# Third blocks of inverses on four array tiles, and state sums with 40 columns of weights, in an RWKV-7 and feed-forward kernel

## The chip, the cores and the metric

The kernel runs on one core of one Trainium2 chip. The metric is the device time of one execution in microseconds. Before the change it is 857.22 us, the median of three runs (856.4 to 857.7); the profiled execution spans 853.2 us.

## The reference

Two parts follow each other. The first is a recurrence over 768 steps of time for 4 batches of 8 heads, with a state of 40 x 40 for each head; the second is a feed-forward layer over the 3072 rows that come out.

```python
def _attn_ref(r, k, v, w, a, b):
    B, H, S, D = r.shape                 # 4, 8, 768, 40
    state = np.zeros((B, H, D, D), dtype=np.float32)
    for t in range(S):
        ...
        y[:, :, t] = np.einsum('bhd,bhde->bhe', rt, state)
        Sa = np.einsum('bhde,bhe->bhd', state, at)
        state_decay = state * wt[:, :, None, :] - np.einsum('bhd,bhe->bhde', Sa, bt)
        state = state_decay + np.einsum('bhd,bhe->bhde', vt, kt)
    return y

def _moe_ref(x, w_in, w_out):            # x: 3072 x 320, w_in: 320 x 2048, w_out: 2048 x 320
    h = x @ w_in
    relu6 = np.clip(h + 3.0, 0.0, 6.0)
    g = h * relu6 / 6.0
    return (g @ w_out).astype(np.float32)
```

All data are fp32 for the kernel's matmuls.

## The kernel before

The kernel cuts time into blocks of 64 steps. A block of two batches and all eight heads is a unit; there are 24 units, four (NU) to a group, and each goes through a preparation (stages W, gam, A, B, F, K, factor, E, EV) and a step (RT, VT, R, C, S, U, UT, rS, sn, H, y, move). Within a block the recurrence is solved with the inverse of a 64 x 64 triangular matrix for each head. That inverse is made in 32 x 32 parts: VectorE builds the inverses of the two diagonal parts for a whole group at once (`invert`), and TensorE makes the part off the diagonal, the third block, as a product of three 32 x 32 matrices, in two bursts of matmuls with an eviction after each. A third block call takes 16 heads (two units); there are twelve calls, the first two of them with `first`. On the 128 partitions lie two 64 x 64 matrices one above the other, x = 0 and 1.

```python
def third_block(F, tb, tt, n, first=False):
    zs = tmp.tile([P, 2 * H, L], F32, name="zs")                     # P = 128, H = 8, L = 32, BL = 64
    parts = [slice(0, H), slice(H, 2 * H)] if first else [slice(0, 2 * H)]
    zp = [ps_any([P, 2 * H, L]) for _ in range(2)]
    for h in range(2 * H):
        for x in range(2):
            z = x * BL
            nc.tensor.matmul(out=zp[x][z:z + L, h, :], lhsT=F[z + L:z + BL, n * H + h, L:BL],   # line 660
                             rhs=tb[z + L:z + BL, n * H + h, :], start=True, stop=True,
                             tile_position=(z + L, z))
    yield PE
    for part in parts:
        for x in range(2):
            z = x * BL
            nc.scalar.activation(out=zs[z:z + L, part], in_=zp[x][z:z + L, part], func=AF.Copy)  # line 667
    ...
    tp = [ps_any([P, 2 * H, L]) for _ in range(2)]
    for h in range(2 * H):
        for x in range(2):
            z = x * BL
            nc.tensor.matmul(out=tp[x][z:z + L, h, :], lhsT=tt[z:z + L, n * H + h, :],           # line 679
                             rhs=zs[z:z + L, h, :], start=True, stop=True,
                             tile_position=(z, z))
    yield PE
    for part in parts:
        heads = slice(n * H + part.start, n * H + part.stop)
        for x in range(2):
            z = x * BL
            nc.scalar.activation(out=tinv[z:z + L, heads, L:BL], in_=tp[x][z:z + L, part],       # line 687
                                 func=AF.Copy)
    yield DONE
```

`tile_position` names the first row and the first column of the part of TensorE's 128 x 128 array that a matmul uses. Both loops over x alternate between two such tiles.

The state's sums of a step (D = 40, SLOT = 64; `half(i)` is the 64 partitions from 64 i):

```python
def s_sn():
    sn = ps_pair(NPR, D)
    for name in "KB":
        for pr in range(NPR):                                        # 4 pairs of heads
            for s in range(2):
                for q in range(2):
                    h = 2 * pr + s
                    by = ...                                         # V or U, 64 x 40
                    nc.tensor.matmul(                                # line 818
                        out=sn[q][half(s), pr, :],
                        lhsT=o[name][half(q), h * D:h * D + SLOT], rhs=by,
                        start=(name == "K" and pr == 0), stop=(name == "B" and pr == NPR - 1))
    yield PE
    for q in range(2):
        nc.vector.tensor_tensor(out=st[:, q, :, 0:D], in0=sn[q], in1=st[:, q, :, 0:D],   # line 825
                                op=ALU.add)
```

The weights of a head are 40 columns wide, but 64 are taken, so 24 columns of the next head come along; their sums go into rows of the state that nothing multiplies with.

Buffers in PSUM: a ring of five banks called "any" for all parts of the recurrence; two banks "h" and one "o" for the feed-forward. `ps_pair` takes two banks at once, one for each row half, and lets several small results share them:

```python
def ps_pair(*dims):
    n = 1
    for d in dims:
        n *= d
    if shared[0] is None or shared[1] + n > 512:
        shared[:] = [ps_any([P, 512]) for _ in range(2)], 0
    at = shared[1]
    shared[1] += n
    ...
    return [_ap(t[:], at, views) for t in shared[0]]
```

Other lines that are spoken of: 420 transposes of inputs, 438 scores (RT with VT or UT), 447 VectorE's mask of the scores, 512 and 534 / 537 the matrix F of the early units and its eviction, 725 the state times a, 763 and 784 U and its transpose, 800 the state's part of the output, 841 the output of a block, 921 and 926 the feed-forward's first product, 931 and 932 its activation on ScalarE and VectorE, 945 its second product. Feed-forward matmuls are fed in between the stages of the recurrence, in pieces, so that TensorE has work while a stage waits for its evictions; the main loop runs a third block between such pieces:

```python
            feed(rate / 2, inversion)
            for _ in parts:
                pass
            if i % NU < 2 and j < 2:
                ...
                block(i, j)              # j = 0: the first burst of a third block, j = 1: the second
            ...
            feed(rate / 2, inversion)
```

Of the kernel before, what the change touches and what calls it, by code (L numbers as in the profile page):

```python
# [8 lines left out]
F32 = mybir.dt.float32  # L9
I32 = mybir.dt.int32  # L10
U32 = mybir.dt.uint32
ALU = mybir.AluOpType
AF = mybir.ActivationFunctionType
# [3 lines left out]
P = 128  # L17
BL = 64
HB = BL // 2
L = 32  # L20
SLOT = 64


def _ap(ap, extra, dims):

    return bass.AP(tensor=ap.tensor, offset=ap.offset + extra, ap=[list(ap.ap[0])] + dims)
# [3 lines left out]
def kernel(  # L30
# [42 lines left out]
    nc = tc.nc  # L73
    B, H, T, D = r.shape
# [13 lines left out]
    tmp = ctx.enter_context(tc.tile_pool(name="tmp", bufs=1))  # L88
# [6 lines left out]
    def bank(tag, shape, bufs):  # L95
        return ps.tile(shape, F32, name=tag, tag=tag, bufs=bufs)
# [3 lines left out]
    def ps_any(shape):  # L100
        tag, bufs = ring[0]
        ring.rotate(-1)
        return bank(tag, shape, bufs)


    shared = [None, 0]
# [10 lines that stand above are left out]
        views, step = [], n  # L117
        for d in dims:
            step //= d
            views.append([step, d])  # L120
        return [_ap(t[:], at, views) for t in shared[0]]
# [6 lines left out]
        out=ident[:], in_=ones, pattern=[[1, P]],  # L128
# [4 lines left out]
        out=ones[:, 0:BL], in_=ones[:, 0:BL], pattern=[[1, BL]],  # L133
# [3 lines left out]
        out=ones[BL:P, 0:BL], in_=ones[BL:P, BL:P], pattern=[[1, BL]],  # L137
# [34 lines left out]
    start = const.tile([P, SCAN], F32, name="start")  # L172
# [24 lines left out]
    tinv = const.tile([P, NH, BL], F32, name="tinv")  # L197
# [183 lines left out]
    PE, DONE = 1, 2  # L381
# [46 lines left out]
    def half(i, n=SLOT):  # L428
        return slice(SLOT * i, SLOT * i + n)
# [221 lines left out]
    def third_block(F, tb, tt, n, first=False):  # L651


        zs = tmp.tile([P, 2 * H, L], F32, name="zs")
        parts = [slice(0, H), slice(H, 2 * H)] if first else [slice(0, 2 * H)]
        zp = [ps_any([P, 2 * H, L]) for _ in range(2)]
        for h in range(2 * H):
            for x in range(2):
                z = x * BL
                nc.tensor.matmul(out=zp[x][z:z + L, h, :], lhsT=F[z + L:z + BL, n * H + h, L:BL],  # L660
                                 rhs=tb[z + L:z + BL, n * H + h, :], start=True, stop=True,
                                 tile_position=(z + L, z))
        yield PE
        for part in parts:
            for x in range(2):
                z = x * BL
                nc.scalar.activation(out=zs[z:z + L, part], in_=zp[x][z:z + L, part], func=AF.Copy)
        if first:
            for part in parts:
                heads = slice(n * H + part.start, n * H + part.stop)  # L670
                for z in range(0, P, BL):
                    nc.gpsimd.tensor_copy(tinv[z:z + L, heads, 0:L], tb[z:z + L, heads])
                    nc.gpsimd.tensor_copy(tinv[z + L:z + BL, heads, L:BL], tb[z + L:z + BL, heads])
        yield DONE
        tp = [ps_any([P, 2 * H, L]) for _ in range(2)]
        for h in range(2 * H):
            for x in range(2):
                z = x * BL
                nc.tensor.matmul(out=tp[x][z:z + L, h, :], lhsT=tt[z:z + L, n * H + h, :],  # L679
                                 rhs=zs[z:z + L, h, :], start=True, stop=True,  # L680
                                 tile_position=(z, z))
        yield PE
        for part in parts:
            heads = slice(n * H + part.start, n * H + part.stop)
            for x in range(2):
                z = x * BL
                nc.scalar.activation(out=tinv[z:z + L, heads, L:BL], in_=tp[x][z:z + L, part],
                                     func=AF.Copy)
        yield DONE


    def step(i):

        n, o = i % NU, data[i]
        g, p = names[i]
        st, dec, VN = state[p], o["dec"], o["VN"]
# [112 lines left out]
# [3 lines that stand above are left out]
                for pr in range(NPR):  # L812
# [3 lines that stand above are left out]
                            by = VN[half(q), 4 * s + pr, 0:D] if name == "K" else \  # L816
                                m["U"][half(q), 4 * (s ^ q) + pr, 0:D]
                            nc.tensor.matmul(  # L818
                                out=sn[q][half(s), pr, :],
                                lhsT=o[name][half(q), h * D:h * D + SLOT], rhs=by,  # L820
                                start=(name == "K" and pr == 0), stop=(name == "B" and pr == NPR - 1),
                            )
            yield PE
            for q in range(2):
                nc.vector.tensor_tensor(out=st[:, q, :, 0:D], in0=sn[q], in1=st[:, q, :, 0:D],  # L825
                                        op=ALU.add)

        def s_H():
            x = scores(m["UT"], m["RT"], swap=True)
# [43 lines left out]
        def s_move2():  # L873
            for dst, src in m["moves"][4:]:
# [4 lines left out]
        return {"RT": s_RT, "R": s_R, "VT": s_VT, "S": s_S, "U": s_U, "C": s_C, "UT": s_UT,  # L879
                "rS": s_rS,  # L880
                "sn": s_sn, "H": s_H, "y": s_y, "move": s_move, "move2": s_move2}


# [123 lines left out]
    third, F, group_F = [], None, []  # L1007
# [54 lines left out]
    n, cleared = 0, []  # L1062
# [12 lines left out]
    while phase[0] in (1, 2, 3):  # L1075
        next(weights)
    firsts = [third_block(*third[-1], n, True) for n in (0, 2)]
    run(firsts[0])
    run(firsts[0], weight=1)

    def block(i, j):

        if i % NU < 2:
            if j == 0:
                n = i % NU
                blocks[i] = third_block(*third[-1], 2 * n)
            run(blocks[i])
# [114 lines left out]
    def a_block(m):  # L1202

        if coming and begins[coming[0]] == m:
            u = coming.popleft()
            close = coming and begins[coming[0]] < m + BLOCKS
            ahead[u, m] = prepared(u), CLOSE_STAGES if close else AHEAD_STAGES
        if m % BLOCKS == 0 and m // BLOCKS + NU < NK:
            i = m // BLOCKS + NU
            own[i, m] = step(i), OWN_STAGES  # L1210
        parts = {}, {}
        for (u, begin), (fs, order) in sorted(own.items()) + sorted(ahead.items()):
            if m - begin < len(order):
                for name in order[m - begin]:
                    parts[begin % BLOCKS > 0].setdefault(name, []).append(fs[name])
        for k, part in enumerate(parts):
            together(part)
            if any(u % NU == NU - 1 and m - begin == 2 and k == (begin % BLOCKS > 0)
                   for u, begin in ahead):
                third.clear()  # L1220
                side.append(invert(group_F[-1], third))
            yield
# [10 lines left out]
    for i in range(NU, NK):  # L1233
        for j in range(BLOCKS):
# [5 lines left out]
            parts = a_block(m)  # L1240
# [51 lines left out]
```

## Time and profile before

| what | value |
|---|---|
| time, median of 3 | 857.22 us |
| span of the profiled execution | 853.2 us |
| mean granted TensorE clock | 0.948 |
| third blocks' matmuls, lines 660 and 679 | 768 + 768, 15.3 + 15.5 us busy |
| state sums' matmuls, line 818 | 1536, 17.0 + 16.3 us busy |
| their additions, line 825 | 48, 13.3 us busy |
| evictions of third blocks, lines 667 and 687 | 28 + 28 |

The profile is one execution, taken by the hardware profiler. Busy time is that of one engine; weight loads are counted apart from matmuls and overlap them. Matmuls are pipelined, so that the time of one matmul in the rows (190 to 230 ns) is mostly latency, and what a burst costs is the distance from one start to the next. "Granted clock" is the share of TensorE's full clock that was allowed. The slices of the page cut the span into 40 equal parts of 21.3 us, a digit being the busy tenths.

### The profile page before, as it was taken

The page shows a single profiled execution, that of the slowest core. Times are in us where ns is not written, and L with a number is a line of the kernel's source. Part 1 is how long each engine was busy: PE and PEld are TensorE (multiplying, and loading weights), DVE is VectorE, ACT ScalarE, POOL GpSimd, SP SyncE. Part 2 cuts the span into 40 slices and gives each one's busy share as a digit, 9 for nine tenths or more (in the row PEclk, how much of TensorE's full clock was granted, in tenths as well). Part 3 has the DMA queues.
Part 4 walks back from the last instruction along what each step waited for, and adds up shares of the span by engine and source line. Part 5 has one row for each costly group of instructions (what it writes and reads, how often), then busy time and mean ns, then how long its engine had stood idle before and what let it go on. Part 6 is the DMA issues. An engine that isn't in the chain of part 4 may idle for free.

```text
span 853.2 us, 34881 instructions
## 1 busy us (share of the span) xinstructions
PE 774.1 (91%) x15480; PEld 660.0 (77%) x15480; DVE 529.4 (62%) x1032; ACT 310.1 (36%) x756; POOL 157.5 (18%) x307
## 2 busy tenths in 40 slices
PE   4723877898999989999999999999999999999998
PEld 3622766776888878888888888888888888888886
DVE  6988598878864579734698454697445674221211
ACT  1322654231344433444324534334453324222111
POOL 3231212112121130221211122113012202000000
PEclk9755878899999999999999999999999999999999
DMA  7572443331123330322231232222232101110000
GB/s 137 86 181 80 112 113 80 64 57 24 33 49 67 59 62 11 61 50 46 46 56 29 43 66 49 45 42 39 41 55 50 18 20 27 25 22 12 17 18 15
DMA packets 174213, 44.99 MB, mean 53 GB/s; under 512 B 157424, under 2 KB 172784, under 8 KB 174064
## 3 DMA queue, kind: packets, MB, share of 16 engines
q1 hardware_dynamic: 171920, 42.44, 26.0%
q8 instruction: 122, 2.00, 1.0%
q10 hardware_dynamic: 2144, 0.33, 0.2%
q14 instruction: 27, 0.22, 0.1%
HBM read 34.08 MB, written 3.93 MB: 45 GB/s over the span
## 4 chain that ended last, share of the span: by engine, by line
PE 78%; DVE 12%; issue 3%; ACT 2%; POOL 1%; DMA 1%; SPq 0%; DVEq 0%; ACTq 0%
PE o L945 24%; PE h L921 20%; PE any L420 6%; PE h L926 5%; PE any L438 3%; PE any L841 3%; PE any L818 3%; DVE prod L626 2%; PE any L660 2%; PE any L679 2%; DVE x L632 2%; PE any L763 2%; PE any L784 1%; PE any L725 1%; PE any L583 1%
## 5 line engine op out<-in xcount | busy, mean ns | idle before, releaser
L945 PE MATMUL o<-wout,gt 128*128 128x320 f32 x768 | 234.8, 449 | 0.0
L921 PE MATMUL h<-xt,win 128*128 128x128 f32 x1536 | 197.6, 283 | 3.2 <-DVE gt L932 3.2
L921 PEld LDWEIGHTS h<-xt,win 128*128 128x128 f32 x1536 | 186.4, 196 | 12.1 <-DVE gt L932 3.9
L945 PEld LDWEIGHTS o<-wout,gt 128*128 128x128 f32 x768 | 139.2, 191 | 54.3 <-issue 1.2
L932 DVE SCALAR_TENSOR_TENSOR gt<-gt,h 128x512 f32<-128x512 f32 x96 | 61.4, 681 | 95.4 <-ACT gt L931 95.4
L931 ACT ACTIVATE gt<-h,three 128x512 f32<-128x512 f32 x96 | 60.8, 684 | 128.0 <-PE h L926 127.8
L856 POOL TENSOR_TENSOR yg<-ys,gam 128x512 f32<-128x512 f32 x24 | 41.3, 1723 | 212.5 <-DVE ys L853 153.9
L626 DVE TENSOR_TENSOR prod<-x 128x30 f32<-128x30 f32 (+9 forms) x180 | 64.1, 356 | 13.4 <-POOL x L617 8.1
L632 DVE TENSOR_TENSOR x<-x,prod 128x30 f32<-128x30 f32 (+9 forms) x180 | 63.9, 355 | 5.5 <-DVE prod L626 0.3
L556 POOL TENSOR_TENSOR KBt<-K,rgt 128x320 f32<-128x320 f32 x24 | 21.6, 899 | 221.6 <-ACT rgt L548 216.3
L926 PE MATMUL h<-xt,win 64*128 64x128 f32 x768 | 55.8, 285 | 0.0
L447 DVE COPY_PREDICATED score<-mask,any 128x256 f32<-128x256 int32 x143 | 53.2, 434 | 1.1 <-PE any L438 1.1
L926 PEld LDWEIGHTS h<-xt,win 64*128 64x128 f32 x768 | 46.6, 187 | 5.2 <-issue 0.3
L474 DVE RECIPROCAL gam<-prods 128x256 f32<-128x256 f32 x24 | 41.5, 1741 | 13.4 <-POOL yg L856 13.1
L825 DVE TENSOR_TENSOR state<-any,state 128x160 f32<-128x160 f32 x48 | 13.3, 319 | 56.0 <-PE any L438 54.5
L489 DVE RECIPROCAL rgam<-prods 128x256 f32<-128x256 f32 x24 | 41.8, 1741 | 0.0
L589 ACT ACTIVATE EV<-any 64x160 f32<-64x160 f32 x92 | 24.8, 295 | 44.4 <-PE any L583 32.6
L463 DVE TENSOR_TENSOR_SCAN prods<-wm,start 128x528 f32<-128x528 f32 x24 | 30.1, 1253 | 16.6 <-ACT wm L460 15.0
L853 DVE TENSOR_TENSOR ys<-any,ys 128x256 f32<-128x256 f32 x44 | 16.6, 418 | 34.5 <-PE any L583 19.9
L704 ACT ACTIVATE RT<-any 128x512 f32<-128x512 f32 x24 | 14.3, 595 | 59.4 <-PE any L420 59.4
L841 PE MATMUL any<-score,KBt 64*64 64x64 f32 x1536 | 31.4, 230 | 2.7 <-DVE score L447 1.6
L841 PEld LDWEIGHTS any<-score,KBt 64*64 64x64 f32 x1536 | 27.3, 142 | 7.6 <-issue 3.3
(184 smaller groups left out, 1137.7 us busy)
## 6 DMA issues: line engine op xcount, KB each, us to landing
B<-in_b_dram SPq DMA_DIRECT2D x48, 80.0 KB
K<-in_k_dram SPq DMA_DIRECT2D x48, 80.0 KB
V<-in_v_dram SPq DMA_DIRECT2D x96, 40.0 KB
out_dram<-ob SPq DMA_DIRECT2D x48, 80.0 KB
R<-in_r_dram SPq DMA_DIRECT2D x92, 40.0 KB
W<-in_w_dram SPq DMA_DIRECT2D x40, 80.0 KB
A<-in_a_dram SPq DMA_DIRECT2D x40, 80.0 KB
xt<-yg SPq DMA_DIRECT2D x72, 40.0 KB
```

What stands on the lines that cost most here:

```text
L420: nc.tensor.transpose(out=o[:, n, :], in_=x[:, 2 * n:2 * n + 2, :].rearrange("p s e -> p (s e)"), identity=ident[:])
L447: nc.vector.copy_predicated(out=x[:, 4 * i:4 * i + 4, :], mask=mask4, data=o[i])
L474: nc.vector.reciprocal(gv[:, :, 0:HB], o["prods"][:, :, 0, 1:HB + 1][:, :, ::-1])
L489: nc.vector.reciprocal(rv[:, :, HB:BL], o["prods"][:, :, 1, 1:HB + 1])
L626: nc.vector.tensor_tensor(out=pv, in0=_ap(x[:], (i + 1) * L + i, [[L, n], [0, i]]), in1=_ap(x[:], i * L, [[0, n], [1, i]]), op=ALU.mult,)
L632: nc.vector.tensor_tensor(out=rest, in0=rest, in1=pv, op=ALU.add)
L841: nc.tensor.matmul(out=y[q][half(s), pr, :], lhsT=o[name][half(q), h * D:h * D + SLOT], rhs=m[name][half(q), 4 * rs + 2 * s + j, :], start ...
L921: nc.tensor.matmul(out=hp[c][:, i, :], lhsT=win[:, t, j * P:(j + 1) * P], rhs=xt[:, t, :], start=(t == 0 and i == 0), stop=False)
L926: nc.tensor.matmul(out=hp[c][:, i, :], lhsT=win2[half(c), (j0 + i) * P:(j0 + i + 1) * P], rhs=xt[half(c), 2, :], start=False, stop=(i == N ...
L931: nc.scalar.activation(out=gt[:], in_=hp[c][:], func=AF.Relu, bias=three[:], scale=1.0)
L932: nc.vector.scalar_tensor_tensor(out=gt[:], in0=gt[:], scalar=6.0, in1=hp[c][:], op0=ALU.min, op1=ALU.mult)
L945: nc.tensor.matmul(out=op[:], lhsT=gts[c][:, n, :], rhs=wout[:, c * HJ + r * NQ + n, :], start=((split or r == 0) and c == 0 and n == 0), ...
```

## The change

Third blocks: heads are taken in twos, y = 0 and 1. The second head's result goes to the other 32 partitions of the same half of PSUM (z + 32), so that the matmuls go round four tiles of the array, two in each row group that is used, and not two. The results of 16 heads then lie in 64 partitions and 8 places of a bank, so an eviction takes four ScalarE instructions with half the elements of the two before (eight and four where `first` is set). They use `ps_pair` in place of two banks of their own; `shared[0] = None` after each burst lets the next user begin new banks. The aim is more matmuls of the small kind at work in the array at the same time.

State sums: only the head's own 40 columns are loaded as weights. The sums then fill 40 of the 64 partitions of a half, so the addition to the state is done for each half by itself: four VectorE instructions on 40 partitions in place of two on 128. The aim is a shorter weight load.

```diff
     def third_block(F, tb, tt, n, first=False):
-        zs = tmp.tile([P, 2 * H, L], F32, name="zs")
-        parts = [slice(0, H), slice(H, 2 * H)] if first else [slice(0, 2 * H)]
-        zp = [ps_any([P, 2 * H, L]) for _ in range(2)]
-        for h in range(2 * H):
-            for x in range(2):
-                z = x * BL
-                nc.tensor.matmul(out=zp[x][z:z + L, h, :], lhsT=F[z + L:z + BL, n * H + h, L:BL],
-                                 rhs=tb[z + L:z + BL, n * H + h, :], start=True, stop=True,
-                                 tile_position=(z + L, z))
+        zs = tmp.tile([P, 2, H, L], F32, name="zs")
+        parts = [slice(0, H // 2), slice(H // 2, H)] if first else [slice(0, H)]
+        zp = ps_pair(H, L)
+        for h in range(H):
+            for y in range(2):
+                for x in range(2):
+                    z = x * BL
+                    g = n * H + 2 * h + y
+                    nc.tensor.matmul(out=zp[x][z + y * L:z + y * L + L, h, :], lhsT=F[z + L:z + BL, g, L:BL],
+                                     rhs=tb[z + L:z + BL, g, :], start=True, stop=True,
+                                     tile_position=(z + L, z + y * L))
         yield PE
         for part in parts:
             for x in range(2):
                 z = x * BL
-                nc.scalar.activation(out=zs[z:z + L, part], in_=zp[x][z:z + L, part], func=AF.Copy)
+                for y in range(2):
+                    nc.scalar.activation(out=zs[z:z + L, y, part], in_=zp[x][z + y * L:z + y * L + L, part],
+                                         func=AF.Copy)
... (the copies of the diagonal parts where `first` is set, on GpSimd, as before)
+        shared[0] = None
         yield DONE
... (the second burst likewise: tile_position (z, z + y * L), four evictions
...  into tinv, which take every other head, and shared[0] = None)

     def s_sn():
...
-                                out=sn[q][half(s), pr, :],
-                                lhsT=o[name][half(q), h * D:h * D + SLOT], rhs=by,
+                                out=sn[q][half(s, D), pr, :],
+                                lhsT=o[name][half(q), h * D:(h + 1) * D], rhs=by,
...
             for q in range(2):
-                nc.vector.tensor_tensor(out=st[:, q, :, 0:D], in0=sn[q], in1=st[:, q, :, 0:D],
-                                        op=ALU.add)
+                for s in range(2):
+                    x = st[half(s, D), q, :, 0:D]
+                    nc.vector.tensor_tensor(out=x, in0=sn[q][half(s, D)], in1=x, op=ALU.add)
```

The number of instructions on TensorE and the order in which all engines take theirs stay as they were, but for the evictions and additions that are split.

More of the change, by code (lines that the diff above doesn't have):

```diff
@@ L666, in third_block @@
                 z = x * BL
-                nc.scalar.activation(out=zs[z:z + L, part], in_=zp[x][z:z + L, part], func=AF.Copy)
+                for y in range(2):
+                    nc.scalar.activation(out=zs[z:z + L, y, part], in_=zp[x][z + y * L:z + y * L + L, part],
+                                         func=AF.Copy)
         if first:
             for part in parts:
-                heads = slice(n * H + part.start, n * H + part.stop)
+                heads = slice(n * H + 2 * part.start, n * H + 2 * part.stop)
                 for z in range(0, P, BL):
@@ L673, in third_block @@
                     nc.gpsimd.tensor_copy(tinv[z + L:z + BL, heads, L:BL], tb[z + L:z + BL, heads])
+        shared[0] = None
         yield DONE
-        tp = [ps_any([P, 2 * H, L]) for _ in range(2)]
-        for h in range(2 * H):
+        tp = ps_pair(H, L)
+        for h in range(H):
+            for y in range(2):
+                for x in range(2):
+                    z = x * BL
+                    nc.tensor.matmul(out=tp[x][z + y * L:z + y * L + L, h, :],
+                                     lhsT=tt[z:z + L, n * H + 2 * h + y, :],
+                                     rhs=zs[z:z + L, y, h, :], start=True, stop=True,
+                                     tile_position=(z, z + y * L))
+        yield PE
+        for part in parts:
             for x in range(2):
                 z = x * BL
[L679 to L688, printed above, removed]
+                for y in range(2):
+                    heads = slice(n * H + 2 * part.start + y, n * H + 2 * part.stop + y - 1, 2)
+                    nc.scalar.activation(out=tinv[z:z + L, heads, L:BL],
+                                         in_=tp[x][z + y * L:z + y * L + L, part], func=AF.Copy)
+        shared[0] = None
         yield DONE
```

## The prediction

> **What bounds the kernel now.** I read the busy table first, then the table of stretches, then the timeline inside the few bursts that the change touches, because a share over the whole span does not say what a nanosecond saved in one stage is worth.
>
> The page's busy line and its slices:
>
> ```profile
> PE 774.1 (91%) x15480; PEld 660.0 (77%) x15480; DVE 529.4 (62%) x1032; ACT 310.1 (36%) x756; POOL 157.5 (18%) x307
> PE   4723877898999989999999999999999999999998
> DVE  6988598878864579734698454697445674221211
> ```
>
> TensorE is busy in 9 tenths of nearly every slice from the tenth on; before that VectorE is the fuller engine and TensorE waits. The table of stretches (columns: length, busy time and count of TensorE, of its weight loads, VectorE, ScalarE, GpSimd, then the granted clock, the DMA share, GB/s) makes it sharper:
>
> ```profile
> 80.00:150.00 70.00, 53.31 (x1444) 47.69 (x1444) 53.62 (x101) 36.27 (x81) 18.89 (x37) 0.79 0.40 95
> ...
> 330.00:400.00 70.00, 70.00 (x1564) 60.31 (x1563) 42.40 (x82) 31.21 (x78) 15.27 (x26) 1.00 0.25 44
> 400.00:470.00 70.00, 70.00 (x1323) 60.33 (x1321) 53.24 (x111) 26.41 (x67) 14.54 (x24) 1.00 0.25 46
> ...
> 715.00:842.00 127.00, 127.00 (x2175) 106.51 (x2176) 27.81 (x65) 31.58 (x68) 6.37 (x11) 1.00 0.09 20
> ```
>
> From about 200 us to 842 us TensorE has no gap to speak of: the only large one in the timeline is 3.23 us at 314 us, before line 725. So in these 640 us time saved on TensorE comes off the end almost one for one, and extra work on VectorE and ScalarE costs nothing unless it lands on a wait. Between 80 and 150 us it is a chain with VectorE at 77% (53.62 of 70) and TensorE at 76%, and little can be said line by line.
>
> Now the bursts (timeline rows: start, length, line, operation, shape, count):
>
> ```profile
> 186.76 1.49 PE L512 MATMUL any<-bt,at 40*32 40x64 f32 x128
> 500.11 1.20 PE L660 MATMUL any<-tb,F 32*32 32x32 f32 x64
> 802.85 0.68 PE L818 MATMUL any<-V,KBt 64*64 64x40 f32 x32
> 803.33 0.66 PE L818 MATMUL any<-U,KBt 64*64 64x40 f32 x32
> 803.80 0.67 PE L438 MATMUL any<-RT,UT 40*64 40x64 f32 x32
> ```
>
> A row's length holds the latency of its last matmul, so I take the distance between starts. Third block (line 660, two array tiles in turn): one matmul is 0.19 us, so (1.20 - 0.19) / 63 = 16.0 ns each; line 679 shows the same in its bursts. State sums (line 818, four tiles): (803.80 - 802.85) / 64 = 14.8 ns each. Line 512 (eight tiles, 32 columns of weights): (1.49 - 0.22) / 127 = 10.0 ns each, at a granted clock of 1.00. That is the quickest burst in the kernel and the best model for what the new code can reach.
>
> [...] loads of 64 columns take 135 ns (line 818), of 32 columns 108 ns (line 660), 27 ns apart[...] in line 818 each row half holds two tiles and yields a matmul every 2 x 14.8 = 29.6 ns[...]. So I let tiles that share rows overlap too. [...]
>
> **The change, part by part.**
>
> Third blocks. The counts stay: a block of 16 heads has two bursts of 64 matmuls (lines 660 and 679), and twelve blocks make 24 bursts, 1536 matmuls. What changes is that a burst goes round four tiles and not two. With two tiles each tile takes a matmul every 2 x 16.0 = 32 ns[...]. If only the tile limited, four would give 8 ns; the quickest burst on the page has 10.0. I take 10. Saving 6 ns x 64 = 0.38 us a burst. Ten blocks, 20 bursts, lie after 200 us: 20 x 0.38 = **7.7 us**.
>
> State sums. 24 steps of 64 matmuls, the weights cut from 64 to 40 columns. If the tile's load is the limit, it now takes 4 x 14.8 = 59 ns a tile[...]. By a straight line between 32 columns at 10.0 (line 512) and 64 at 14.8 it would be 11.2. I choose 10.5. Saving 4.3 x 64 = 0.28 us a step; 20 steps lie after 200 us: **5.5 us**.
>
> What it adds. Each eviction of a third block becomes twice as many ScalarE instructions of half the length. ScalarE has 587 ns for 32x512 (lines 667, 687) and 376 ns for 32x256 (line 537): 2 x 587 = 1174 becomes 4 x 376 = 1504 ns, 0.33 us more, 20 times, 6.6 us on an engine that is busy 36%. In the steady stretch a block's matmuls are followed by feed-forward matmuls (line 945 at 501.24 above), and its result is asked for half a block later, so this is beside TensorE's work. Two PSUM banks are held 0.3 us longer, of a ring of five. Nothing for the path.
>
> The state's addition becomes four VectorE instructions on 40 partitions where two on 128 stood. The free size, 160, is the same, so I give each the 316 ns of the old ones: 48 x 316 = 15 us more busy time. A pair took 0.56 us in the timeline, so four take about 1.04: the mask behind it (line 447) ends 0.48 us later. In the last steps that mask ends at 805.76 us and its matmuls (line 841) start at 808.54: 2.8 us to spare. Nothing for the path, but for the stretch at 314 us where line 725 waits for VectorE, and for its like at 562 us (0.22 us). I take off 1.2 us for such places.
>
> Early part, 80 to 150 us. Two blocks at a lower clock, in a chain: matmuls, eviction, matmuls, eviction, with almost no work beside. Each of the four bursts may lose 0.5 to 0.7 us on TensorE; each eviction goes from 4 x 373 to 8 x about 265 ns (line 534, 32x128), 0.6 us more. Four state sums add 4 x 0.48 = 1.9 us to VectorE's queue, where the weights' conversion also waits. I call it even.
>
> Sum: 7.7 + 5.5 - 1.2 = **12.0 us** off 857.2, so 845.2 us, 1.4% less.
>
> **The rivals.**
>
> (a) The row group is the limit, not the tile. Both bursts still use two row groups, so third blocks would keep 16 ns and only the sums gain: 852 us. [...] Against: line 818's 29.6 ns per row half, and line 512's 20 ns per row half with the same 32 columns.
>
> (b) About 14.5 ns is a floor of the four-tile form, whatever the columns: lines 763, 784 and 818 start their matmuls 15.3, 15.6 and 14.8 ns apart, though the moving side has 40, 64 and 40 columns. Then the sums gain nothing and third blocks 1.5 x 64 x 20 = 1.9 us: 856 us. Against: all those have 64 columns of weights, and line 512 is at 10.0.
>
> (c) The evictions become the bound. The four ScalarE and four VectorE instructions stand in front of what the feed-forward needs (lines 931 and 932), whose two PSUM buffers TensorE waits for. TensorE waited for line 932 only twice, 3.2 us in all, so there is slack; but in the early chain each 0.5 us would show. I would give this 2 to 5 us at the worst: 848 to 850 us.
>
> (d) Everything goes well: 8 ns for third blocks (20 x 64 x 8 = 10.2 us), 9.8 for the sums (6.4 us) and 1.5 us early: 839 us.
>
> **Range and chances.** The two pitches carry the spread. With 12 ns for both, the gain is 5.1 + 3.6 = 8.7, less 3 for the early chain, 5.7 us, 851.5 us; at the other end (d). I take 839.5 to 851 as the eight-in-ten range. Two per cent is 17.1 us, below 840.1: it needs nearly all of (d), 0.12. Slower by 2% would need a fault that nothing here shows, 0.02.
>
> **What would show it.** In the timeline after: a third-block burst of 64 in about 0.82 us ((63 x 10) + 190 ns), not 1.20; a step's state sums with 0.67 us between the first start and the next line's first, not 0.95; four ScalarE rows of some 376 ns behind each steady third-block burst; four VectorE rows of some 316 ns in each state addition. In the stretches after 200 us TensorE should still have no gaps, and each stretch should end earlier by its share of 13 us; the early part should reach the feed-forward's steady run at about the same time. The prediction fails if either pitch stays at its old value (a or b), if new gaps open before lines 763, 841 or 921 (c), or if the early chain slips by more than 3 us.

## The result and the profile after

The changed kernel takes 848.99 us (median of 4 runs, 848.88 to 849.13) against 856.81 us: 0.9906 of the kernel before, with a 95% interval of 0.9892 to 0.992. That is 7.8 us less; 12.0 were predicted. The profiled executions span 847.2 and 853.2 us.

The page of the changed kernel, busy time and slices:

```profile
PE 763.3 (90%) x15480; PEld 648.0 (76%) x15480; DVE 549.3 (65%) x1080; ACT 318.3 (38%) x812; POOL 156.7 (18%) x307
...
PE   4623876898999989999999999999999999999997
...
DVE  6998697988964669844599654698546684232211
```

TensorE's busy time fell by 11 us and VectorE's rose by 20, with 48 instructions more. The table of stretches (columns as before):

```profile
80.00:150.00 70.00, 52.78 (x1409) 47.41 (x1409) 53.20 (x101) 37.34 (x95) 17.14 (x35) 0.68 0.38 91
...
330.00:400.00 70.00, 69.70 (x1612) 59.22 (x1605) 46.03 (x91) 33.66 (x91) 15.25 (x26) 1.00 0.24 44
400.00:470.00 70.00, 70.00 (x1326) 60.33 (x1325) 55.33 (x114) 24.84 (x62) 13.70 (x22) 1.00 0.25 46
...
715.00:836.00 121.00, 120.39 (x2086) 100.58 (x2085) 28.92 (x67) 30.90 (x70) 6.36 (x11) 1.00 0.08 19
```

Two things differ from before: 35 matmuls fewer are done between 80 and 150 us, at a granted clock of 0.68 and not 0.79; and TensorE is no longer without gaps (69.70 of 70, 120.39 of 121). The timeline of TensorE, a third block's two bursts and a step's state sums:

```profile
498.64 0.75 PE L662 MATMUL any<-tb,F 32*32 32x32 f32 x64
499.32 1.34 PE L955 MATMUL o<-wout,gt 128*128 128x320 f32 x4
...
504.98 0.81 PE L685 MATMUL any<-zs,tt 32*32 32x32 f32 x64
...
796.93 0.51 PE L827 MATMUL any<-V,KBt 64*40 64x40 f32 x32
797.26 0.50 PE L827 MATMUL any<-U,KBt 64*40 64x40 f32 x32
797.56 0.68 PE L438 MATMUL any<-RT,UT 40*64 40x64 f32 x32
```

The two third-block bursts take 0.75 and 0.81 us and not 1.20: (0.75 - 0.19) / 63 = 8.9 ns a matmul, (0.81 - 0.19) / 63 = 9.8. Of the 20 bursts after 200 us, eleven go at 8.9 ns and nine at 9.6 to 12.5. These sums take (797.56 - 796.93) / 64 = 9.8 ns, not 14.8; to the nanosecond, the trace has 9.9 or 10.5 in the steps after 200 us, where the kernel before has 14.9. (A row's count is of the profile's records; each of these fp32 matmuls of the program leaves two: x64 in a burst of 32.) So the bursts did what they were meant to do, and a little more. The timeline of VectorE behind the same step's sums, before:

```profile
804.52 0.56 DVE L825 TENSOR_TENSOR state<-any,state 128x160 f32<-128x160 f32 x2 [1.92 <-PE any L438]
805.00 0.76 DVE L447 COPY_PREDICATED score<-mask,any 128x256 f32<-128x256 int32 x2
```

and after:

```profile
798.29 1.33 DVE L836 TENSOR_TENSOR state<-any,state 40x160 f32<-40x160 f32 x4 [1.60 <-PE any L438]
799.63 0.77 DVE L447 COPY_PREDICATED score<-mask,any 128x256 f32<-128x256 int32 x2
```

Two additions held VectorE for 805.00 - 804.52 = 0.48 us; the four hold it for 799.63 - 798.29 = 1.34.

**Where the time went.** TensorE's matmuls come in the same order in both kernels, so the two traces can be laid side by side, matmul by matmul, and the change of each distance between starts put down to its line. After 200 us: third blocks -8.25 us, state sums -6.08, everything else +5.2 in new waits; sum -9.2. At 200 us the changed kernel is 2.9 us behind. (These two executions differ by 6.0 us in span, the medians by 7.8.) The first third-block burst after 200 us is a good mark for the early part: it starts at 227.23 us in the kernel before and at 229.43 in the changed one.

### The profile page after: what moved, and what is told of

Read it like the earlier page. It is cut to its first block, busy times and chain, and to the rows that moved or that the text cites. A ratio compares the mean times of both kernels' runs of the same rounds, so it can differ in the third digit from the quotient of the medians.

```text
span 847.2 us, 35021 instructions
## 1 busy us (share of the span) xinstructions
PE 763.3 (90%) x15480; PEld 648.0 (76%) x15480; DVE 549.3 (65%) x1080; ACT 318.3 (38%) x812; POOL 156.7 (18%) x307
## 4 chain that ended last, share of the span: by engine, by line
PE 76%; DVE 12%; issue 4%; SPq 3%; ACT 2%; POOL 2%; DMA 1%; DVEq 0%; POOLq 0%; ACTq 0%
PE o L955 24%; PE h L931 21%; PE any L420 6%; PE h L936 5%; PE any L438 4%; PE any L851 3%; PE any L827 2%; DVE prod L626 1%; PE any L772 1%; PE any L734 1%; DVE x L632 1%; PE any L793 1%; PE any L583 1%; PE any L809 1%; DVE gam L474 1%
## 5 line engine op out<-in xcount | busy, mean ns | idle before, releaser
L931 PEld LDWEIGHTS h<-xt,win 128*128 128x128 f32 x1536 | 187.3, 197 | 14.3 <-DVE gt L942 6.3
L836 DVE TENSOR_TENSOR state<-any,state 40x160 f32<-40x160 f32 x96 | 30.8, 321 | 51.6 <-PE any L438 49.6
L474 DVE RECIPROCAL gam<-prods 128x256 f32<-128x256 f32 x24 | 41.5, 1741 | 13.5 <-POOL yg L866 13.2
L713 ACT ACTIVATE RT<-any 128x512 f32<-128x512 f32 x24 | 14.3, 594 | 57.2 <-PE any L420 57.2
```

Of the source, the lines that this page charges most:

```text
L474: nc.vector.reciprocal(gv[:, :, 0:HB], o["prods"][:, :, 0, 1:HB + 1][:, :, ::-1])
L931: nc.tensor.matmul(out=hp[c][:, i, :], lhsT=win[:, t, j * P:(j + 1) * P], rhs=xt[:, t, :], start=(t == 0 and i == 0), stop=False)
```

## The experiments

Theory A: VectorE's doubled additions and ScalarE's doubled evictions stand on the path, above all early, where VectorE converts the feed-forward's weights, which arrive as 64-bit numbers, to fp32 almost without a pause (until 158.4 us in the kernel before). Theory B: the early loss is TensorE's clock, and the late waits are TensorE running ahead of the supply of its own instructions. "Mark" below is the start of the first third-block burst after 200 us, in one execution of each kernel. The ratio is to executions of the kernel before from the same session, whose medians were 855.7 to 856.8 us.

| kernel | ratio to before | 95% interval | mark, us |
|---|---|---|---|
| before | 1 | | 227.23 |
| changed | 0.9906 | 0.9892 to 0.992 | 229.43 |
| third blocks alone | 0.9907 | 0.988 to 0.9934 | 225.81 |
| state sums alone | 1.0011 | 0.9999 to 1.0023 | 229.67 |
| changed, early work old | 0.9873 | 0.9847 to 0.9899 | 226.18 |
| changed, K with 64 columns, two additions | 0.989 | 0.9854 to 0.9926 | 226.30 |
| changed, additions' loops exchanged | 0.9907 | 0.9876 to 0.9939 | 229.94 |
| third blocks everywhere, 40 columns late | 0.987 | 0.9836 to 0.9904 | 224.77 |
| the same with K 64, B 40 late | 0.988 | 0.9846 to 0.9914 | 226.59 |
| changed, stream moved by 128 instructions | 0.9906 | 0.988 to 0.9932 | 231.03 |
| before, additions split | 1.0075 | 1.0057 to 1.0094 | 231.55 |
| before, evictions split | 1.0026 | 1.0011 to 1.004 | 225.69 |
| 40 columns late, stream moved | 0.9865 | 0.9841 to 0.989 | 225.38 |

**Each part alone.** The diff of the change was taken for one part only; the other function stays as in the kernel before.

> The changed third blocks with the old state sums (64 columns, two additions). The aligned traces give, after 200 us, 8.25 us less in the third blocks' bursts and 6.1 us less in the sums'; 5.2 us come back as new waits and the early part ends 2 to 2.7 us later. Theory A, the split evictions and additions bring the waits, each part its own: this keeps the early loss of the first blocks, no waits of the state's additions, 851 to 852 us. Theory B, TensorE at times outruns the supply of its instructions, and the early loss is one of the clock: gaps in the middle of bursts become fewer but don't vanish, 852 to 853.5 us. If the early loss belongs to the state sums, 849.5 to 850.5 us.

> The changed state sums with the old third blocks. Theory A: no waits for the longer evictions of third blocks, the early part as before if the loss is of the first blocks: 851 to 852 us, and the first third-block burst after 200 us starts at about 227 us. Theory B: 852 to 854 us with one or two gaps inside bursts. If the early loss belongs to the sums' four additions in VectorE's queue, that burst starts at about 229 us and the time is 853 to 854 us. This and the kernel with third blocks alone should add up to the full change if the parts are independent: the two gains sum to 7.8 us.

Third blocks alone give the whole gain, 0.9907; the state sums alone give nothing, 1.0011, though their bursts after 200 us were 6.1 us shorter, as in the changed kernel. In both, the nearest of the expectations was the one that puts the early loss on the four additions. The mark at 229 us fits; the times went further than expected, third blocks alone to some 848.8 us on the scale of 856.8 (849.5 to 850.5 expected) and the sums alone to 857.8 (853 to 854). With third blocks alone the mark is early, so the first third blocks aren't behind the loss. In the aligned traces the new waits after 200 us are 2.1 us with third blocks alone and 3.2 with the sums alone: together they are the 5.2 of the changed kernel. The timeline of VectorE before:

```profile
123.69 0.69 DVE L312 TENSOR_TENSOR win<-raw_fb,parts 128x512 f32<-128x512 f32 x1
124.31 0.55 DVE L825 TENSOR_TENSOR state<-any,state 128x160 f32<-128x160 f32 x2
124.77 0.68 DVE L320 SCALAR_TENSOR_TENSOR parts<-raw_tt,parts 128x512 uint32<-128x512 uint32 x1
```

and with the state sums alone:

```profile
124.74 0.69 DVE L312 TENSOR_TENSOR win<-raw_fb,parts 128x512 f32<-128x512 f32 x1
125.35 1.32 DVE L827 TENSOR_TENSOR state<-any,state 40x160 f32<-40x160 f32 x4
126.70 0.69 DVE L320 SCALAR_TENSOR_TENSOR parts<-raw_tt,parts 128x512 uint32<-128x512 uint32 x1
```

No bracket stands behind these rows: VectorE has no pause here. The next conversion starts 0.46 us after the additions' start before, and 1.35 us after it here: 0.89 us more, on the engine that is the fuller one (100 to 160 us, sums alone: VectorE busy 51.14 of 60 us, TensorE 44.57). Over four early units that would be 3.6 us at most (an estimate from these rows). TensorE's waits before:

```profile
PE h L921 <- DVE gt L932: 3.2, 2, 3.0
PE any L841 <- DVE score L447: 1.6, 1, 1.6
```

and with the state sums alone (the same two waits, and the two lines have moved by one):

```profile
PE h L922 <- DVE gt L933: 5.3, 2, 4.0
...
PE any L842 <- DVE score L447: 2.3, 2, 2.1
```

The longest wait of the feed-forward's first product grows from 3.0 to 4.0 us, that of the block's output from 1.6 to 2.1. In all five kernels with doubled additions in the early units the first of these is 3.8 to 4.0 us, in the other eight 1.5 to 3.0.

**The early work in its old form.**

```diff
-    firsts = [third_block(*third[-1], n, True) for n in (0, 2)]
+    firsts = [old_block(*third[-1], n, True) for n in (0, 2)]
-                "sn": s_sn, ...
+                "sn": old_sn if i < NU else s_sn, ...
```

> The changed kernel, but the two first third blocks and the state sums of the first four units in their old form; all work after 200 us is as in the changed kernel. If the early loss of 2 to 2.7 us comes from the changed early work (longer evictions in a chain, or less of TensorE's clock), the first third-block burst after 200 us starts at about 227 us and the time is 846 to 847 us. If it is only where the clock's windows happen to fall, it stays at 849 us.

0.9873, with the mark at 226.18 us: the early loss goes with the early work. Its interval just touches that of the changed kernel, so that it is the faster one rests on the mark as well.

**Two additions again, half the shorter loads.**

```diff
+                            c = SLOT if name == "K" else D
-                                out=sn[q][half(s, D), pr, :],
-                                lhsT=o[name][half(q), h * D:(h + 1) * D], rhs=by,
+                                out=sn[q][half(s, c), pr, :],
+                                lhsT=o[name][half(q), h * D:h * D + c], rhs=by,
...
+                nc.vector.tensor_tensor(out=st[:, q, :, 0:D], in0=sn[q], in1=st[:, q, :, 0:D], op=ALU.add)
```

> The changed kernel, but in the state sums the K half loads 64 columns again and only the B half 40, so that all 128 partitions are written and the addition is again two VectorE instructions. Gives back half of the sums' gain, 3.0 us, and takes 16 us of VectorE's busy time away. If the doubled additions are behind the waits, 848 to 850 us, with the wait at 560 us and the early loss smaller; if VectorE's time lies beside the path, as was predicted, 851.5 to 852.5 us.

The sums' bursts after 200 us gain 2.9 us and not 6.1, yet the time is 0.989, not slower, and the mark is at 226.30. In the aligned traces this kernel gains 10.5 us after 200 us, the changed one 9.2. The doubled additions cost at least what half the shorter loads bring.

**Splitting the additions in the kernel before.** The cost by itself: no matmul differs.

```diff
             for q in range(2):
-                nc.vector.tensor_tensor(out=st[:, q, :, 0:D], in0=sn[q], in1=st[:, q, :, 0:D], op=ALU.add)
+                for s in range(2):
+                    x = st[half(s), q, :, 0:D]
+                    nc.vector.tensor_tensor(out=x, in0=sn[q][half(s)], in1=x, op=ALU.add)
```

> The kernel before with nothing changed but the state's addition, which is split into four VectorE instructions on 64 partitions (same sums, same matmuls). The cost of the split by itself. If VectorE's queue in the early part is what ate the state sums' gain, TensorE's bursts after 200 us start 3 to 5 us later and the time is 1.004 to 1.007 of the kernel before; if the split lies beside the path, 1.000 to 1.002.

1.0075 (1.0057 to 1.0094), some 6 us, and the mark is 4.3 us late; after 200 us only 1.3 us are added. No matmul differs, so the split alone does this, and it costs about what the shorter loads save (6.1 us). The loss builds up at the additions. Those of the last early unit, before:

```profile
149.01 0.55 DVE L825 TENSOR_TENSOR state<-any,state 128x160 f32<-128x160 f32 x2
```

and those of the last two with the additions split:

```profile
125.20 1.32 DVE L827 TENSOR_TENSOR state<-any,state 64x160 f32<-64x160 f32 x4
151.87 1.34 DVE L827 TENSOR_TENSOR state<-any,state 64x160 f32<-64x160 f32 x4
```

The second early unit's additions still start on time (101.86 us, 102.01 before); the third's start 0.89 us late, the fourth's 2.86, and the last conversion of a weight ends at 162.13 us and not at 158.37. In the eight kernels without doubled early additions it ends at 157.3 to 159.3 us, in the four that have them in this order at 162.1 to 163.0.

The rival is the clock of Theory B. Between 100 and 160 us the granted clock is 0.80 before, 0.74 in the changed kernel, 0.72 with the sums alone, 0.83 with third blocks alone. But the kernel with K at 64 columns and two additions, and then the kernel before with its additions split, show in that stretch (columns as before):

```profile
100.00:160.00 60.00, 44.76 (x887) 39.09 (x888) 51.85 (x95) 27.21 (x59) 9.11 (x17) 0.77 0.42 98
100.00:160.00 60.00, 42.98 (x904) 37.34 (x897) 51.34 (x96) 26.38 (x55) 9.71 (x19) 0.76 0.42 98
```

Nearly the same clock, and marks of 226.30 and 231.55 us; the changed kernel with the additions' loops exchanged (below) has 0.76 and 229.94. So the clock doesn't make this difference; that it has some smaller share isn't excluded.

**Splitting the evictions in the kernel before.** Twice the parts in `for part in parts` of both evictions.

> The kernel before with nothing changed but the third blocks' evictions, which are split into twice as many ScalarE instructions of half the length. If they lie beside the path, as was predicted, 1.000 to 1.001 of the kernel before; if ScalarE's queue holds TensorE back by the 0.4 to 0.5 us that the changed kernel shows near 268 us at each of several places, 1.002 to 1.004.

1.0026 (1.0011 to 1.004), some 2 us. I had predicted that they are free; they cost a third of what the additions do. The mark is not late (225.69 us); 2.1 us are added after 200 us. One place of it is plain in the changed kernel's waits after 200 us:

```profile
PE any L438 <- ACT UT L800: 0.5, 1, 0.5
```

Near 268 us a third block's four evictions stand in ScalarE's queue in front of those of U and UT, which TensorE wants next.

**The order of the four additions.**

```diff
-            for q in range(2):
-                for s in range(2):
+            for s in range(2):
+                for q in range(2):
```

> The changed kernel with the two loops of the state's addition exchanged: the four additions start on partitions 0, 0, 64, 64 and not 0, 64, 0, 64. In the changed kernel four took 1.32 us, 0.335 us from start to start, so they don't overlap, where two on 128 partitions were 0.24 us apart. If an addition that starts on other partitions than the one before is held until that has ended, only two of four are held now: start to start 0.24, 0.33, 0.24 us, four in about 1.15 us, and the time falls by some of 24 x 0.17 us: 847 to 848.5 us. If the number of instructions is what counts, four still take 1.32 us and the time is 849.

The timeline of VectorE for it:

```profile
797.89 1.13 DVE L836 TENSOR_TENSOR state<-any,state 40x160 f32<-40x160 f32 x4 [1.60 <-PE any L438]
799.03 0.78 DVE L447 COPY_PREDICATED score<-mask,any 128x256 f32<-128x256 int32 x2
```

Four take 1.14 us and not 1.34: from start to start 0.24, 0.32 and 0.25 us, where all were some 0.335. An addition takes 0.32 us. So additions on the same start partition overlapped (0.24 and 0.25 us apart), and one that starts elsewhere began when the one before had ended (0.32 to 0.335 us apart). The last conversion of a weight ends at 160.86 us and not at 162.25. The time doesn't show it: 0.9907, and the mark is still late, 229.94. Four early units with 0.2 us less of VectorE each should have shown a little; that they don't is open.

**Forty columns only after the conversion.** Third blocks changed everywhere, `old_sn` for the first four units, the exchanged loops after; then the same with K 64, B 40 after.

> Third blocks changed everywhere, state sums old for the first four units (where VectorE converts the weights) and with 40 columns and the exchanged loops after. If the early loss is that of VectorE's queue, the first third-block burst after 200 us starts at 225 to 226 us as with third blocks alone, and the late bursts bring their whole gain: 842 to 844 us. If the early loss is the clock's, it starts at 228 us or later and the time is 846 to 848 us.

> As the last, but the later units load 64 columns for K and 40 for B and add with two VectorE instructions. Half the sums' gain, 3 us less than the last in TensorE's bursts, but none of the 1.1 us wait of line 921's like at 560 us and no doubled additions. If VectorE's additions cost more than 3 us after 200 us, this is the quicker one, 841 to 843 us; if less, it is 1 to 2 us slower than the last.

0.987 and 0.988, some 845.7 and 846.5 us, both slower than their forecasts (842 to 844 and 841 to 843). The intervals overlap, so which of the two is better can't be told. The marks, 224.77 and 226.59 us, differ by 1.8 us though the code ahead of them is the same; so a mark scatters by that much at least. The marks of the five kernels with early doubled additions (229.4 to 231.6) lie beyond those of the eight without (224.8 to 227.2).

**The stream of instructions.** Three of the late gaps in the changed kernel lie in the middle of a burst, where no engine is waited for. The timeline of one:

```profile
741.26 0.42 PE L809 MATMUL any<-RT,S 40*64 40x64 f32 x16
742.26 0.46 PE L809 MATMUL any<-RT,S 40*64 40x64 f32 x16 [0.58 <-issue]
```

Counted through the trace from 0, semaphore rows included, the loads and matmuls behind these gaps are numbers 12481, 24001 and 28609 of TensorE; each is 193 over a multiple of 256. The six other kernels with changed third blocks and no move have such gaps at one or both of 24001 and 28609 too. The page has a DMA queue that fits (packets, MB, share of 16 engines):

```profile
q8 instruction: 122, 2.00, 1.0%
```

2.00 MB in 122 pieces are 16.4 KB each, and TensorE's 31,400 or so rows over 122 are 257. In the trace of the changed kernel a piece lands 1.2 to 1.4 us before each of the three gaps ends.

```diff
+    dummy = bank("o", [P, DM], 1)
+    for n in range(32):
+        nc.tensor.matmul(out=dummy[0:L, 0:L], lhsT=ident[0:L, 0:L], rhs=ident[0:L, 0:L], start=True, stop=True)
```

> The changed kernel with 32 small matmuls more at the very start, where TensorE waits for its first inputs: 128 TensorE instructions (64 loads, 64 matmuls) that move all later ones in the instruction stream. The gaps inside bursts of the changed kernel (0.3 us at 368.8, 0.56 at 631.4, 0.58 at 742.3) lie in front of instructions 12481, 24001 and 28609 of the trace, all 193 over a multiple of 256. If they are TensorE waiting for its next block of 256 instructions, they vanish from there and any that remain are again 193 over a multiple, in front of other instructions; the time moves by up to 2 us either way. If they come from waits for other engines, they stay in front of the same matmuls, at remainder 65.

All three are gone. One new one inside a burst stands near 491 us:

```profile
490.05 0.29 PE L441 MATMUL any<-at,kt 40*64 40x64 f32 x5
490.74 0.68 PE L441 MATMUL any<-at,kt 40*64 40x64 f32 x27 [0.40 <-issue]
```

It lies in front of number 17857: again 193 over a multiple of 256, and in the unmoved kernel there was no gap at this matmul. Gaps that wait for an engine (the 3.2 us near 318 us) stayed with their matmuls. So Theory B is right for these gaps in that they belong to a place in the stream of instructions. That TensorE waits there for its next piece of 256, which the shorter bursts sometimes need too early, is my reading of the 193, the 257 rows a piece and the landing 1.2 to 1.4 us before; the wait itself stands in no trace. The move is worth about 1.2 us after 200 us in the aligned traces (-10.35 against -9.16); the time, 0.9906, is the same, since this run's early part ended later (mark at 231.03).

> Third blocks changed everywhere, state sums with 40 columns only after the first four units, and the 32 small matmuls at the start that move the instruction stream by 128. If the gaps inside bursts (0.67 us at 626 and 0.71 at 737 in the run without the move) are the supply of instructions, they go, and this is 1 to 1.5 us quicker than that: about 0.985 of the kernel before, the best so far.

0.9865 (0.9841 to 0.989), the lowest of all, with no gap of this kind left after 200 us, and 10.8 us gained there against 8.5 without the move. That it is faster than without the move is in the trace only; the two intervals overlap. They overlap with that of third blocks alone too, which gain 6.3 us after 200 us.

## Why the prediction was right, and where it was not

The time, 849.0 us, lies inside the range of 839.5 to 851. The sum of 12.0 us was too large. Its gains were not at fault: 13.2 us were predicted after 200 us, and the bursts lost 14.3. Two of the costs that it took off or left out were too small: 1.2 us for waits and nothing for the early part stood against 5.2 and 2.9. That the time still fell inside is owed to the width of the range, whose slow end had 3 us for the early part, and not to the estimate of these costs.

- *What bounds the kernel.* Right in the main after 200 us, but not "almost one for one": of the 14.3 us that the bursts lost there, 9.2 reached the end.
- *Third blocks, 10 ns.* 8.9 ns in eleven of 20 bursts, 8.25 us in all against 7.7: near the 8 ns of "if only the tile limited". Rival (a), the row group as the limit, is refuted by the trace: with four tiles in two row groups, a row group took a matmul every 2 x 8.9 = 17.8 ns, where it took one every 2 x 16.0 = 32 ns with two. So tiles that share rows did work side by side, which the prediction had assumed.
- *State sums, 10.5 ns.* 9.9 to 10.5 ns, 6.1 us against 5.5. The straight line between two measured bursts gave 11.2; that it would be less, and the 9.8 of (d), were my estimates. The loads in the trace before, 135 ns for 64 columns and 108 for 32, give nearly the same: 20 ns less for 24 columns, 59 - 20 = 39 ns a tile, 9.7 each (an estimate). Rival (b), a floor at 14.5 ns for four tiles, is refuted.
- *VectorE's additions, "nothing for the path", and the early part, "I call it even".* This is the step that failed, twice over. The size: a pair's 0.56 us was doubled to 1.04, as if four would overlap like two; but they alternate between partitions 0 and 64 and don't, so the extra is 0.86 us and not 0.48. The length of one was as predicted, 322 ns for 40x160 against 316 for 128x160; the distance between starts was not, 0.335 us when alternating and 0.24 when not. And the place: the early part was called a chain, but 1.9 us more in VectorE's queue were set against TensorE's shorter bursts as if they cancelled. VectorE runs almost without a pause there (before, busy 52.16 of the 60 us from 100 to 160), so its extra time reached the mark. Splitting the additions alone costs 0.75%, and 4.3 of its 6 us or so are there by the mark.
- *Early third blocks, even.* Somewhat better: with third blocks alone the mark is 1.4 us ahead, within what marks scatter.
- *ScalarE's evictions, nothing for the path.* Too small: 0.26% when added alone.
- *No gaps after 200 us.* This sign failed. Of the 5.2 us of new waits, 0.5 is ScalarE near 268 us; 0.9 near 275 us (line 583's products wait for a mask that stands behind the four additions) and 0.9 near 560 us are VectorE; and 2.0 are the three gaps inside bursts, which the prediction didn't think of. The rest, some 0.9 us, is spread over small places.
- *Rival (c).* It named VectorE's queue in front of line 932 and line 921's wait for it, and 2 to 5 us, 848 to 850, at the worst: the size fits. But line 921's longest early wait grew by 1.0 us only, so it is a part of the early loss and not all of it.

## What to carry to other kernels

An engine's slack has to be read in the stretch where the extra work falls: the same four additions were free at 800 us, where TensorE didn't wait for them, and put off what followed on VectorE by their extra 0.89 us at 125 us, where VectorE had no pause. When a smaller result splits an instruction by partitions, count the pieces as if nothing overlaps: here those that alternated between partitions 0 and 64 came 0.335 us apart at 0.32 us each, and the split by itself cost as much as the shorter weight loads saved. Let it wait until the crowded stretch is over; the kernels that do so are at 0.9865 to 0.988, though only the lowest lies clear of the changed kernel's interval. And try each half of a double change alone: one half was the whole gain.

## What the runs showed of the hardware that was not expected

- TensorE's matmuls of 32 columns on 32 rows start 8.9 ns apart in most bursts when four tiles in two row groups take turns (9.6 to 12.5 in the others), 16.0 ns with two tiles.
- TensorE stopped inside bursts without a wait for an engine: three gaps of 0.3 to 0.6 us in the changed kernel, each 193 over a multiple of 256 in the count of its instructions, went from their places when 128 instructions were put in front, and the new one, 0.4 us, lay at 193 again. That it is the supply of instructions is my reading.
- VectorE additions that started on other partitions than the one before didn't overlap with it: 0.32 to 0.335 us from start to start, 0.24 otherwise, for 160 elements and 0.32 us of each.
